# Late modulation columns and one token load moved in a fused transformer block

## The chip, the cores and the metric

The kernel runs on one core of a Trainium2 chip. The metric is the device time of one execution in microseconds; lower is better. An execution works on five engines with queues of their own: TensorE (matmul, PE), VectorE (DVE), ScalarE (ACT), GpSimd (POOL), and SyncE (SP), which here only issues DMAs. An engine starts its instructions in the order of its queue; semaphores order the engines among each other.

## The reference, cut to what matters

One transformer block over 2048 tokens of width 1024, with all its modulation computed from one condition vector `c`:

```python
mod = (silu(c) @ w_mod).reshape(1, 6, 1, -1)       # w_mod: 1024 x 6144
sa, ca, ga, sb, cb, gb = six rows of 1024
h = layernorm(x) * (1 + ca) + sa
q = (h @ wq), 32 heads of 128                       # wq: 1024 x 4096
p = softmax(q @ k.T * 128**-0.5)                    # the last 512 keys, 4 key heads
x = x + ga * ((p @ v) @ wo)                         # wo: 4096 x 1024
h = layernorm(x) * (1 + cb) + sb
x = x + gb * ((silu(h @ w_gate) * (h @ w_up)) @ w_down)   # width 3584
```

Everything is bfloat16 outside, with float32 sums.

## The kernel before, in words

The tokens are cut into four chunks of 512. Attention runs over 128 items, an item being one head of one chunk: item i belongs to chunk i // 32 and head i % 32. The loop at line 1007 writes the program out in order, and every engine gets its instructions in that order. In turn i it emits the query projection of item i + 3 (eight matmuls into one PSUM bank, then VectorE's cast to SBUF, line 675), the scores of item i - 1 (four matmuls into four banks, then the exponential on ScalarE, line 848), and the value product of item i - 2 (16 small matmuls, then a reciprocal and a multiplication on VectorE, lines 866 and 869). SP then transposes the product by DMA (line 872) into `oT_all`, from which the output projection reads it. From item 34 on, every second item takes another form: scores with queries on the partitions (line 909), normalisation on VectorE (lines 915 and 919), a transposing DMA of the probabilities (line 925), and a value product that lands transposed (line 936).

At a seam, the end of turns 33, 65 and 97, the chunk that is through gets its output projection, `oproj`: eight blocks k of 32 matmuls each, one matmul per head, into two banks in turn. Matmul h of a block reads `oT_all[:, h]`. Behind each block VectorE multiplies by the gate row and adds to the residual (lines 950 and 952). The last chunk's projection is spread over the end of the loop. The gated feed-forward of all chunks follows.

The rows `gb`, `sb` and `cb` of the modulation are wanted late. They are computed on VectorE during the first chunk's projection, 128 values at a time. A "late column" m (24 of them) is a block of `w_mod` that SP loads transposed into one of four slots (`load_mt`, line 592; slot m % 4), and that VectorE multiplies by the broadcast silu(c) and sums (`mod_col`, line 601, with the instruction at line 604). The slots lie in the buffer that held chunk 0's normalised tokens. `late_cols(k)`, line 608, is called behind block k of the first projection. It runs three columns, and behind each column m it issues the load of column m + 4 into the slot that is now free. At k = 3 the first eight columns, the gate `gb`, are turned by DMA; they go out as a row at k = 4 and come back broadcast at k = 5. At k = 7 the other sixteen are copied into the modulation table (line 629) and the gain is made (line 478).

Tables in front of the loop set which turn issues which DMA. `LOADT` issues the first four late-column loads, behind the value product of its turn. `LOADX` issues the 1 MB token loads of chunks 2 and 3 at the head of a turn; these tokens are wanted when the layer norm of their chunk starts, two turns behind a seam. `PUTT` and `GETT` store a small row to DRAM and fetch it back broadcast to all partitions; the fetch waits for the store. Query weights (1 MB, `load_wq`, line 363) are loaded every four items. All of these, like all transposes, stand in SP's one queue.

Of the kernel before, what the change touches and what calls it, by code (L numbers as in the profile page):

```python
# [130 lines left out]
def bass_adaLN_cond__sliding_block_cached__swiglu_ffn__prompt_kernel(  # L131
# [17 lines left out]
    Hq = HD // Dh  # L149
# [117 lines left out]
    with nc.Block() as block:  # L267

        @block.gpsimd
        def _(g):  # L270
# [82 lines left out]
            def wq_slot(gidx):  # L353
                return gidx if gidx <= NWQ else (gidx + 1) % NWQ
# [3 lines left out]
            def load_wq(gidx):  # L358
                if gidx >= NCH * HG:
                    return  # L360
                sl = wq_slot(gidx)
                hg = gidx % HG
                T.op(Q_wq[sl], lambda: SP.dma_start(
                    wq_s[sl], A_wq[:, hg * 512:(hg + 1) * 512].rearrange("(k p) n -> p k n", p=P)), writes=B_wq[sl])
# [219 lines left out]
            NL = NJ - NF  # L584
            NMT = 4
# [6 lines left out]
            def load_mt(m):  # L592
                sl = m % NMT
                n = L_ORDER[m]
                if mt[sl] is None:
                    mt[sl] = arena.at(OFF_HT + 2 * sl * KB, [D], BF16, [B_mt[sl]])
                T.op(Q_mt[sl], lambda: SP.dma_start_transpose(
                    mt[sl].rearrange("p (a b) -> p a b", a=1), w_mod[:, (NF + n) * P:(NF + n + 1) * P]),
                     writes=[B_mt[sl]])

            def mod_col(m):
                sl = m % NMT
                n = L_ORDER[m]
                T.op(DVE, lambda: V.scalar_tensor_tensor(mt[sl], mt[sl], 1.0, sc_row, op0=ALU.mult, op1=ALU.mult,  # L604
                                                         accum_out=mcol[:, n:n + 1]),
                     reads=[B_scr], writes=[B_mt[sl], B_mcol])

            def late_cols(k):
                for m in range(3 * k, 3 * k + 3):
                    mod_col(m)  # L610
                    if m + NMT < NL:
                        load_mt(m + NMT)
                if k == 3:
                    T.op(DVE, lambda: V.tensor_copy(mstg[:, 0:DT], mcol[:, 2 * DT:3 * DT]), reads=[B_mcol], writes=[B_mstg])
                    row_turn()
                if k == 4:
                    row_put(2, mrow[0:DT, :], B_mrow)
                if k == 5:
                    row_get(2, rowb[1][:, :], B_row[1])
                if k == 7:  # L620
                    for g0 in range(2):
                        mod_take(g0, B_late[g0 + 1])
                    mod_gain(1, B_late[2], B_g[1])
                    for b_ in B_hT[0]:
                        for m_ in B_mt:
                            b_.absorb(m_)

            def mod_take(g0, cbuf):
                T.op(DVE, lambda: V.tensor_copy(mod_bf[:, NF + g0 * DT:NF + (g0 + 1) * DT], mcol[:, g0 * DT:(g0 + 1) * DT]),
                     reads=[B_mcol], writes=[cbuf])  # L630
# [7 lines left out]
            def row_put(r, src, sbuf):  # L638
                T.op(Q_dr[r], lambda: SP.dma_start(d_rows[r:r + 1, :].rearrange("o (k p) -> (o k) p", p=P), src),
                     reads=[sbuf], writes=[B_dr[r]])  # L640

            def row_turn():
                T.op(Q_turn, lambda: SP.dma_start_transpose(mrow.rearrange("p (a b) -> p a b", a=1), mstg),
                     reads=[B_mstg], writes=[B_mrow])

            def row_get(r, dst, dbuf):
                rep_ap = bass.AP(tensor=d_rows.tensor, offset=r * D, ap=[[0, P], [1, D]])
                T.op(Q_rw[r], lambda: SP.dma_start(dst, rep_ap), reads=[B_dr[r]], writes=[dbuf])
# [344 lines left out]
                ln2[ch] = ln_task(ch, h2s[s], B_h2[s], 1, 3 * DT, B_late[1])  # L993
                bg.append(ln2[ch])

            LOADX = {19: 2, 40: 3}
            GATEP = {4: (0, 1), 5: (2,), 6: (3,), 7: (4,), 9: (5,), 10: (6,), 12: (7,), 13: (8,), 15: (9,)}
            GATER = {19 + n: NGP + n for n in range(DT - NGP)}
            GATET = {23: 0, 24: 1}
            GATES = {26: 0, 27: 1}  # L1000
            PUTT = {22: (0, c_sil, B_csil), 30: (1, mrow[0:DT, :], B_mrow)}
            GETT = {25: (0, sc_row, B_scr), 31: (1, rowb[0][:, :], B_row[0])}
            LOADT = {30: 0, 31: 1, 32: 2, 33: 3}
            LOADO = {5 + (21 * p) // 8: p for p in range(8)}
            LOADK = {1: 1, 5: 2, 6: 3}
            PTAT = {NAT0: OFF_H20, 3 * Hq: OFF_HT}
            for i in range(1, NA + 2):
                ch, h = divmod(i, Hq)
                if i in LOADK:
                    load_k(LOADK[i])  # L1010
                if i == 4:
                    load_wq((i + 4) // 4 + 1)
                if 2 <= i < NQ0:
                    q_shifted(i)
                if i in (2, 3):
                    load_wga(i - 2)
                if i in LOADX:
                    load_x(LOADX[i])
                if i in LOADO:
                    load_wo(LOADO[i])  # L1020
                if i in GATET:
                    gate_turn(GATET[i])
                if i == 28:
                    row_turn()
                if i in PUTT:
                    row_put(*PUTT[i])
                if i in GETT:
                    row_get(*GETT[i])
                if i == 7:
                    add_ln1(1)  # L1030
                if h == 2 and 1 <= ch < NCH - 1:
                    add_ln1(ch + 1)
                if h == 2 and ch == NCH - 1:
                    add_ln2(0)
                if i + LEAD < NA:
                    if (i + LEAD) % Hq == 0:
                        finish(ln1[(i + LEAD) // Hq])
                    if i == 1:
                        scores(0)
                    if i in (1, 3, 5):  # L1040
                        q_bias_mm(i + 1, i + 3, XB)
                    if i > NQ0:
                        qproj(i + LEAD)
                    elif i % 2 == 1:
                        qproj_mm(NQ0 + i // 2, QB, 0, HK)
                    else:
                        qproj(NQ0 - 1 + i // 2, QB, HK)
                if i % 4 == 0 and i > NAT0:
                    load_wq(i // 4 + 2)
                n = i - (NA - LEAD)  # L1050
                if 0 <= n <= 2:
                    oproj_mm(NCH - 1, 0, QB, 8 * n, 8 * n + 8)
                elif n >= 3:
                    oproj_mm(NCH - 1, 1, XB, 8 * (n - 3), 8 * (n - 3) + 8)
                seam = (i - 1) % Hq == 0 and i + 1 in NAT
                if i + 1 in PTAT and not seam:
                    pt_region(PTAT[i + 1])
                if i in NAT and (i - 2) % Hq:
                    nat_norm(i, 1)
                nat = i % 2 == 1 and i + 1 in NAT  # L1060
                if nat and not seam:
                    run_bg(1)
                    nat_scores(i + 1)
                if 1 <= i - 1 < NA and i - 1 not in NAT:
                    scores(i - 1)
                if 0 <= i - 2 < NA:
                    if i - 4 in pt_of:
                        nat_pv(i - 4)
                    if i in NAT and (i - 2) % Hq:
                        nat_turn(i)  # L1070
                    if i - 2 not in NAT:
                        pv(i - 2)
                    if nat and not seam:
                        nat_norm(i + 1, 0)
                    ch2, h2 = divmod(i - 2, Hq)
                    if i % 4 == 1 and 5 < i < NAT0:
                        load_wq((i + 4) // 4 + 1)
                    if i in LOADT:
                        load_mt(LOADT[i])
                    if h2 == Hq - 1 and ch2 < NCH - 1:  # L1080
                        oproj(ch2, [lambda: nat_scores(i + 1), lambda: (nat_norm(i + 1, 0), nat_norm(i + 1, 1))],
                              [n for n in sorted(pt_of) if n // Hq == ch2])
                        if seam:
                            if i + 1 in PTAT:
                                pt_region(PTAT[i + 1])
                            nat_turn(i + 1)
                if not nat or seam:
                    run_bg(1)
                for n in GATEP.get(i, ()):
                    gate_part(n)  # L1090
                if i in GATER:
                    gate_row(GATER[i])
                if i in GATES:
                    gate_sum(GATES[i])
                if i == max(GATER):
                    gate_split()
# [154 lines left out]
```

## Time and profile before

| what | value |
|---|---|
| three runs, median (lowest to highest) | 1273.71 us (1272.12 to 1275.35) |
| the profiled execution's own time | 1273.79 us |
| its span, first to last instruction | 1271.9 us |
| mean granted TensorE clock | 0.999 |
| VectorE, late columns (line 604) | 24 of 1222 ns, 29.3 us busy, first at 146.6, last at 198.4 |
| SP, transposed late-column loads (line 597) | 24, issue 1160 / 1169 / 2885 ns (least, median, most), landing 3.3 / 3.7 / 6.7 us after the start of issue |
| SP, attention transposes into `oT_all` (line 872) | part of 109 transposes from and into the arena, 3.9 us to landing |
| token loads of 1 MB (line 308) | 3, issued at 26.6, 90.7 and 222.1, landing 7.0, 7.1 and 6.0 later |
| first seam's projection | first residual addition (line 950) at 145.28, last at 194.42 |

Busy time is the time in which an engine works on an instruction. The view of waits lists who stood idle and which instruction ended the wait (total, times, longest). The chain of waits is followed back from the last instruction. In the timeline a DMA's issue stands in SP's queue with the time that the issuing took; when the data land is told apart from it. The windows view gives, for each stretch, its length, the busy time (and instructions) of PE, PEld, DVE, ACT and POOL, then the granted clock, the DMA share and GB/s.

### The profile page before, as it was taken

Reading aid. Unit: us, or ns where it says so; the run is one execution under the profiler, and the core shown is the slowest. Engines: PE = TensorE matmul, PEld = TensorE weight load, DVE = VectorE, ACT = ScalarE, POOL = GpSimd, SP = SyncE. Lnnn points to the kernel's source line nnn. Section 1 sums busy time; section 2 is a strip of 40 time slices with the busy share of each in tenths; the row PEclk is TensorE's granted clock in tenths of the full one; section 3 lists DMA queues with packets and bytes.
Section 4 is the critical chain, followed back from the end, with each engine's and each line's share of the span. In section 5 each row is a group of like instructions: output and inputs, shape, how many; then the busy total and the mean of one; then the engine's idle time right before and its main releaser. Section 6 shows DMA issues by size and latency. Waiting matters only on the chain.

```text
span 1271.9 us, 17309 instructions
## 1 busy us (share of the span) xinstructions
PE 1263.1 (99%) x7019; PEld 617.1 (49%) x7019; DVE 518.9 (41%) x1081; ACT 392.7 (31%) x718; POOL 55.9 (4%) x95
## 2 busy tenths in 40 slices
PE   9999999999999999999999999999999999999999
PEld 5655544555445554455544444444444444444444
DVE  5676577664246652376422321233212331222222
ACT  4655304775037771177710111011100111011100
POOL 1530000000000000000000000000000000000000
PEclk9999999999999999999999999999999999999999
DMA  9999666987029872099543973055411644035200
GB/s 313 266 269 222 151 132 132 216 186 151 18 41 201 168 179 41 1 191 195 99 146 100 289 223 117 25 156 151 149 58 57 191 141 132 17 118 164 67 9 26
DMA packets 312191, 175.14 MB, mean 138 GB/s; under 512 B 205488, under 2 KB 298032, under 8 KB 312112
## 3 DMA queue, kind: packets, MB, share of 16 engines
q1 hardware_dynamic: 253856, 115.31, 40.0%
q10 hardware_dynamic: 58256, 58.73, 14.6%
q8 instruction: 55, 0.90, 0.3%
q14 instruction: 24, 0.20, 0.1%
HBM read 119.93 MB, written 4.20 MB: 98 GB/s over the span
## 4 chain that ended last, share of the span: by engine, by line
PE 98%; DVE 1%; DMA 0%; issue 0%; ACT 0%; DVEq 0%; ACTq 0%
PE ps L277 98%; DVE st L430 0%; DVE arena L604 0%; DMA x_res<-in_A_x_dram 0%; DVE arena L869 0%; PE ps L281 0%; DVE arena L675 0%; ACT tmp L909 0%; DVE arena L701 0%; DVE tmp L950 0%; DVE nsc L441 0%; DVE tmp L919 0%; DVE x_res L952 0%; DVE mv L530 0%; DVE rl L866 0%
## 5 line engine op out<-in xcount | busy, mean ns | idle before, releaser
L277 PE MATMUL ps<-arena 128*128 128x512 bf16 (+1 forms) x6774 | 1257.1, 348 | 6.1 <-DVE arena L675 3.1
L277 PEld LDWEIGHTS ps<-arena 128*128 128x128 bf16 x6774 | 608.4, 98 | 648.7 <-issue 5.3
L848 ACT ACTIVATE arena<-ps 128x1024 bf16<-128x1024 f32 x160 | 163.7, 1023 | 229.9 <-PE ps L277 222.5
L1179 ACT ACTIVATE arena<-ps 128x512 bf16<-128x512 f32 x112 | 66.9, 597 | 501.0 <-PE ps L277 498.1
L1180 DVE TENSOR_TENSOR arena<-ps,arena 128x512 bf16<-128x512 f32 x112 | 77.4, 691 | 276.2 <-PE ps L277 276.2
L950 DVE TENSOR_TENSOR tmp<-ps,rowb 128x512 f32<-128x512 f32 (+1 forms) x65 | 44.4, 683 | 292.2 <-PE ps L277 292.2
L675 DVE CAST arena<-ps 128x512 bf16<-128x512 f32 x120 | 82.8, 690 | 77.9 <-PE ps L277 77.9
L909 ACT ACTIVATE arena<-ps 128x512 bf16<-128x512 f32 x96 | 56.9, 595 | 26.3 <-PE ps L277 21.9
L909 ACT ACTIVATE tmp<-ps 128x512 bf16<-128x512 f32 x92 | 54.5, 595 | 25.8 <-PE ps L277 21.6
L869 DVE TENSOR_TENSOR arena<-ps,rl 128x512 bf16<-128x512 f32 x81 | 56.0, 691 | 3.0 <-DVE rl L866 0.2
L435 POOL TENSOR_SCALAR rstd<-mv 128x1 f32<-128x1 f32 x28 | 6.1, 216 | 913.5 <-DVE mv L434 913.5
L866 DVE RECIPROCAL rl<-ps 128x4 f32<-128x4 f32 x81 | 14.7, 182 | 73.9 <-PE ps L277 73.9
L430 DVE BATCH_NORM_STATS2 st<-x_res 128x6 f32<-128x512 bf16 x62 | 42.4, 683 | 3.5 <-DMA x_res<-in_A_x_dram 3.4
L919 DVE TENSOR_SCALAR arena<-arena,pinv 128x512 bf16<-128x512 bf16 x96 | 33.9, 353 | 3.4
L936 ACT ACTIVATE arena<-ps 128x512 bf16<-128x512 f32 x47 | 27.8, 592 | 19.6 <-PE ps L277 19.6
L919 DVE TENSOR_SCALAR tmp<-tmp,pinv 128x512 bf16<-128x512 bf16 x92 | 32.5, 353 | 3.3
L604 DVE SCALAR_TENSOR_TENSOR arena<-arena 128x1024 bf16<-128x1024 bf16 x24 | 29.3, 1222 | 1.7
L952 DVE TENSOR_TENSOR arena<-tmp,x_res 128x512 bf16<-128x512 f32 (+2 forms) x33 | 22.3, 676 | 1.1
L952 DVE TENSOR_TENSOR x_res<-tmp,x_res 128x512 bf16<-128x512 f32 x32 | 22.1, 692 | 1.1
L446 DVE TENSOR_SCALAR arena<-arena,gain,mod_bf 128x512 bf16<-128x512 bf16 x56 | 21.2, 420 | 0.0
L441 DVE TENSOR_SCALAR nsc<-x_res,mv,rstd 128x1024 bf16<-128x1024 bf16 x30 | 19.2, 641 | 0.0
L909 ACT ACTIVATION_READ_ACCUMULATOR arena<-ps 128x1 f32 x96 | 18.9, 197 | 0.0
(67 smaller groups left out, 149.4 us busy)
## 6 DMA issues: line engine op xcount, KB each, us to landing
arena<-in_A_wq_dram SPq DMA_DIRECT2D x30, 1024.0 KB, 6.0
arena<-in_B_w_gate_dram ACTq DMA_DIRECT2D x28, 1024.0 KB, 5.5
arena<-in_B_w_up_dram ACTq DMA_DIRECT2D x28, 1024.0 KB, 8.2
arena<-in_A_wo_dram SPq DMA_DIRECT2D x8, 1024.0 KB, 7.6
arena<-in_B_w_down_dram SPq DMA_DIRECT2D x7, 1024.0 KB, 8.5
out_dram<-arena SPq DMA_DIRECT2D x15, 256.0 KB, 2.0
x_res<-in_A_x_dram SPq DMA_DIRECT2D x3, 1024.0 KB, 7.0
arena<-in_w_mod_dram SPq DMA_DIRECT2D x8, 256.0 KB, 5.8
```

What stands on the lines that cost most here:

```text
L277: T.op(PE, lambda: TE.matmul(out_ap, lhsT, rhs, start=start, stop=stop, skip_group_check=skip), reads=reads, writes=[bank_buf])
L430: T.op(DVE, lambda: V.bn_stats(st_[sl][:, hf * 6:hf * 6 + 6], x_res[:, t, hf * 512:hf * 512 + 512]), reads=[B_x[t]], writes=[B_st[sl]])
L604: T.op(DVE, lambda: V.scalar_tensor_tensor(mt[sl], mt[sl], 1.0, sc_row, op0=ALU.mult, op1=ALU.mult, accum_out=mcol[:, n:n + 1]), reads=[B_ ...
L675: T.op(DVE, lambda: V.tensor_copy(qT_s[qs], bank(b)), writes=[PB[b], B_qT[qs]])
L848: T.op(ACT, lambda: A.activation(ex_s[es][:, 2 * kp:2 * kp + 2, :], banks2(SCB + 2 * kp), AF.Exp, scale=att_scale), writes=[PB[SCB + 2 * k ...
L869: T.op(DVE, lambda: V.tensor_tensor(o_s[os_].rearrange("p (a b) d -> p a b d", a=2), psap(PVB * 512, [[512, 2], [130, 2], [1, P]]), rlb, A ...
L909: T.op(ACT, lambda: A.activation(pn[s][:, j * 512:(j + 1) * 512], bank(SCB + j), AF.Exp, scale=att_scale, accum_out=psum[s][:, j:j + 1]), ...
L919: T.op(DVE, lambda: V.tensor_scalar(pj, pj, pinv[s][:, j:j + 1], None, op0=ALU.mult), reads=[B_pinv[s][hf]], writes=[B_pn[s][hf]])
L950: T.op(DVE, lambda: V.tensor_tensor(tmp[s][:, 0:n], bank(b, n), rowb[ri][:, c0:c0 + n], ALU.mult), reads=[B_row[ri]], writes=[PB[b], B_tmp ...
L952: T.op(DVE, lambda: V.tensor_tensor(dst[:, c0:c0 + n], tmp[s][:, 0:n], x_res[:, t, c0:c0 + n], ALU.add), reads=[B_tmp[s], B_x[t]], writes= ...
L1179: T.op(ACT, lambda: A.activation(sg_s[ss], bank(gb), AF.Silu), writes=[PB[gb], B_sg[ss]])
L1180: T.op(DVE, lambda: V.tensor_tensor(guT[:, ft, :], bank(ub), sg_s[ss], ALU.mult), reads=[B_sg[ss]], writes=[PB[ub], B_gu[ft]])
```

## The change

- `late_cols(k)` no longer does anything behind block 7. Block 0 runs four columns (2 to 5), blocks 1 to 6 three each (6 to 8, up to 21 to 23). The copies into the modulation table and the gain move from block 7 to block 6.
- Columns 0 and 1 run in turns 32 and 33 of the item loop, behind the query projection and ahead of the scores, each followed at once by the load of column m + 4 (4 and 5).
- `LOADT` starts one turn earlier: loads 0 to 3 go out in turns 29 to 32 instead of 30 to 33.
- `LOADX` moves the token load of chunk 3 from turn 40 to turn 65, the turn of the second seam.

```diff
+            def late_col(m):
+                mod_col(m)
+                if m + NMT < NL:
+                    load_mt(m + NMT)
+
             def late_cols(k):
-                for m in range(3 * k, 3 * k + 3):
-                    mod_col(m)
-                    if m + NMT < NL:
-                        load_mt(m + NMT)
+                if k < 7:
+                    for m in range(3 * k + (3 if k else 2), 3 * k + 6):
+                        late_col(m)
...
-                if k == 7:
+                if k == 6:
                     for g0 in range(2):
                         mod_take(g0, B_late[g0 + 1])
...
-            LOADX = {19: 2, 40: 3}
+            LOADX = {19: 2, 2 * Hq + 1: 3}
...
-            LOADT = {30: 0, 31: 1, 32: 2, 33: 3}
+            LOADT = {29: 0, 30: 1, 31: 2, 32: 3}
...
                 if i % 4 == 0 and i > NAT0:
                     load_wq(i // 4 + 2)
+                if i in (Hq, Hq + 1):
+                    late_col(i - Hq)
                 n = i - (NA - LEAD)
```

## The prediction

> **What bounds the kernel now.** The page first: TensorE is busy 1263.1 of 1271.9 us, and the clock row of the slices is 9 throughout. What is left to win is TensorE's idle time, plus what a slower clock behind such a pause costs.
>
> ```profile
> PE 1263.1 (99%) x7019; PEld 617.1 (49%) x7019; DVE 518.9 (41%) x1081; ACT 392.7 (31%) x718; POOL 55.9 (4%) x95
> ```
>
> The view of waits, for TensorE alone, says where the idle time lies. Of the 8.8 us, 3.0 lie in the first 46 us and 2.4 behind the last matmul, untouched. The longest of the others is 2.9 us on line 675, VectorE's cast of a projected query from PSUM.
>
> ```profile
> PE ps L277 <- DVE arena L675: 3.1, 2, 2.9
> ...
> PE ps L277 <- ACT tmp L909: 0.2, 1, 0.2
> PE ps L277 <- DVE pinv L915: 0.2, 1, 0.2
> ```
>
> The chain of waits says why that cast was late (start, duration, what):
>
> ```profile
> 194.42 0.70 DVE tmp L950
> ...
> 195.15 0.69 DVE x_res L952
> 195.84 1.16 DVE arena L604 x2
> ...
> 199.69 0.25 DVE mod_bf L629 x2
> ...
> 200.05 0.69 DVE arena L675
> 200.74 0.05 issue
> 200.79 5.29 PE ps L277 x28
> ```
>
> Block 7 of the first output projection ends at 194.40. VectorE adds it to the residual, then runs the last three late columns (line 604) and the copies behind them, and only then casts item 37's query, from 200.05. Item 38's projection needs that PSUM bank, so TensorE stands still for 2.91 us, from 197.88 to 200.79. The windows view, cut where the granted clock changes, shows the aftermath: after a stretch with TensorE busy 0.63 of 3.42 us, the next runs at clock 0.50 and gets through eight matmuls.
>
> ```profile
> 197.25:200.67 3.42, 0.63 (x12) 0.45 (x8) 3.25 (x9) 1.38 (x2) 0.00 (x0) 1.00 0.00 0
> 200.67:204.08 3.41, 3.29 (x8) 1.19 (x9) 1.44 (x4) 0.00 (x0) 0.00 (x0) 0.50 0.20 38
> ```
>
> **Part 1, the stall removed.** The change leaves block 7 without a column. VectorE's queue after that block is then 0.69 + 0.69 (lines 950, 952) to 195.84, and the cast of item 37 follows as soon as its projection, eight matmuls after 194.4, is out: about 196.15 to 196.85, ahead of the 197.88 at which TensorE wants the bank. Gain 2.91. The eight matmuls behind it took 427 ns each in the slow window; at full clock a block of 32 takes 6.91 us (line 950 at 187.51 and 194.42), 216 ns each, so 8 x 0.211 = 1.69 more. What is late next there? The scores of item 36 need ScalarE to have emptied the four score banks (two exponentials, 196.58 to 198.72); TensorE reaches them at 197.88 + 1.73 = 199.6. That is 0.9 us of cover. The 0.16 us wait on line 915 at 208.7 is VectorE catching up after the stall; bounds 0 and 0.16, and I take it all, since VectorE will be 4 us ahead there.
>
> The Trainium skill ("TensorE: Matmul & The Clock Gate", Part 1) has the clock fall after a whole idle window of about 3.4 us. Here 2.91 us of idling, within one 3.42 us stretch that was not wholly idle, were followed by clock 0.50. By the page's rule the 1.69 would not be recovered and the sum below would be -1.7; the row decides.
>
> **Part 2, two columns before the seam.** Columns 0 and 1 move to items 32 and 33, ahead of the normalisation of items 30 and 31 in VectorE's queue. A column is 1.22 and its accumulator read, 1.25 in a row of them. In these items VectorE idles 0.82 and 1.08 us per head (line 675 and line 866 rows), so the column fits but for 0.2 us, and 0.7 if its weights land at 134.2 (below). TensorE's next value product starts near 137.4, and the line 869 that frees its banks ended at 135.72: 1.7 us of cover. Cost nothing; with the cover gone, 1.25 a column. POOL has nothing queued there: it idles for 104.2 us up to 205.96. Blocks 0 to 6 then carry 4 + six times 3 columns. Block 0 needs 1.4 + 5.0 and block 6 1.4 + 3.8 + 0.4 us of VectorE, within 6.91. Block 1 adds item 34's normalisation (1.8) to 1.4 + 3.8, about 0.1 over, covered by the alternating bank.
>
> **Part 3, SP's queue before the first seam.** This is the cost that matters. Transposed weight loads (line 597) are issued by SP in order, and the attention transposes (line 872) stand between them.
>
> ```profile
> 126.54 1.50 SPq L363 DMA_DIRECT2D arena<-in_A_wq_dram  x1
> 128.09 0.48 SPq L639 DMA_DIRECT2D mod_rows<-arena  x1
> 128.75 1.20 SPq L872 DMA_TRANSPOSE arena<-arena  x1
> 129.99 1.92 SPq L597 DMA_TRANSPOSE arena<-in_w_mod_dram  x1
> 133.73 0.36 SPq L648 DMA_DIRECT2D rowb<-mod_rows  x1
> 134.13 1.20 SPq L872 DMA_TRANSPOSE arena<-arena  x1
> 135.38 1.30 SPq L597 DMA_TRANSPOSE arena<-in_w_mod_dram  x1
> 136.72 1.26 SPq L872 DMA_TRANSPOSE arena<-arena  x1
> 138.03 1.30 SPq L597 DMA_TRANSPOSE arena<-in_w_mod_dram  x1
> 139.37 1.26 SPq L872 DMA_TRANSPOSE arena<-arena  x1
> ```
>
> The last line is item 31's transpose, out 0.1 us after its data were ready; it landed 2.5 us later, at 141.9. From the row fetch at 133.73 on, SP has no pause: it is the bound already. Block 0 needs it for its 32nd matmul, near 145.05 (line 950 starts at 145.28), so slack is 3.1 us. Now load 0 goes out right behind the query weights at 128.1, and loads 3, 4 and 5 are issued ahead of item 31's transpose too. The row fetch waits for the little row store of line 639, which landed with the query weights (issue 126.54, landing 6.8 later: 133.3) at 133.7. It now stands behind load 0 also, and the load that went out right behind query weights at 141.30 landed 0.84 after them: so 133.3 + 0.84 + 0.35 = 134.5. From there: 0.40 (fetch) + 1.25 (item 29) + 2 x 1.34 (loads 2, 4) + 1.31 (item 30) + 2 x 1.34 (loads 3, 5) = 8.32, so item 31's transpose goes out at 142.9 instead of 139.4. Its landing, 2.5 (its own row) to 3.4 us (item 30's), comes at 145.4 to 146.3. TensorE waits 0.35 to 1.25; I take 0.75. Outer bounds: 0 if the fetch is not delayed and the landing is quick; 2.0 with the slowest such landing here, 4.0 us (item 29's). In both, load 4 waits for column 0 (done by 135.5) and load 5 for column 1 (138.6); SP reaches them at 137.5 and 141.5: no wait. Load 0's buffer was last read by item 31's projection, cast from 119.48: no wait either.
>
> **Part 4, the last tokens.** The 1 MB load of chunk 3 leaves item 40 (issue 222.13, landing 6.0 later). Behind it stands the 0.2 us wait on line 909 at 235.7; bounds 0 and 0.21, I take 0.21. It arrives at item 65, ahead of item 63's transpose in SP's queue:
>
> ```profile
> 305.46 0.54 SPq L363 DMA_DIRECT2D arena<-in_A_wq_dram  x1
> 306.75 4.41 SPq L925 DMA_TRANSPOSE arena<-tmp  x1
> 311.25 1.22 SPq L872 DMA_TRANSPOSE arena<-arena  x1
> ```
>
> That last one landed 2.5 later, at 313.7; block 0 of chunk 1 needs it near 317.0 (its line 950 starts at 317.23). Now the 1 MB load goes out at 311.2 and lands at 317.2 (6.0, as at 222.13). The transpose behind cannot overtake it: chunk 2's load at 90.75 took 7.1 us, and the transpose issued 0.68 behind it landed 0.7 after it. So 317.2 + 0.6 to 0.7 = 317.8: a wait of 0.8. Bounds: 0.3 (load 5.7, as quick query weights) to 2.5 (load 7.1, transpose 1.26 behind, as at 114.91). The tokens themselves are wanted 55 us later. These two waits are far shorter than 2.91; the trace has a pause of 0.5 us (10.67 to 11.16) at full clock and nothing between. I charge no slow clock, 1.7 each at worst.
>
> **The sum.** -2.91 - 1.69 - 0.16 - 0.21 + 0.75 + 0.8 = -3.4 us. The profiled execution took 1273.79, its span 1271.9 with 1.9 around it, and the runs' median is 1273.71, so both bases agree: 1270.3. Nothing under 0.3% (3.8 us) can be told from no change here.
>
> **Rivals.**
> *No new wait (0.23).* Both transposes land in time, as their 3.1 and 3.3 us of slack might allow if the DMA queues run faster than the rows say: 1273.79 - 4.97 = 1268.8. Against it: SP's row of issues has no pause to give back.
> *SP's queue stretches (0.15), slower.* The load at 141.30 behind 1 MB of query weights took 2.88 us to issue, not 1.34. Should loads 1 to 5 all go out so, since SP now pushes six of them into the same ring, item 31's transpose is 5 x 1.54 = 7.7 later than forecast; TensorE waits 8.4 and pays a slow window: -4.97 + 8.4 + 1.7 + 0.8 = +5.9, 1279.7. It turns slower once that wait passes 2.5 us, slow window included. For it: 1.92 and 2.88 in the rows; against: three loads in a row during the projection took 1.16 to 1.17 each, with no 1 MB load among them.
> *Another wait takes the cast's place (0.10).* ScalarE's exponentials or VectorE's next casts hold TensorE as long, the clock falls as before, and only the two small waits are gained: 1273.79 - 0.37 + 1.55 = 1275.0. Against: the 0.9 us of cover, and no wait in the same rhythm at 236 to 400 us, where TensorE is busy 164.0 of 164.0.
>
> The forecast has 0.52, its own range being 1269.0 to 1272.0. Faster by over 0.3% means under 1269.9: the first rival and not quite half of the forecast, 0.46. Slower by over 0.3%: nearly all of the second, 0.14. The rest is 0.40. The range runs from 1267.8 (first rival less 1 us between runs) to 1275.0 (third rival) and leaves out the second.
>
> **What would show it.** Part 1: no line 604 between lines 952 and 675 at the end of the first seam, no clock under 1.00 after the start. Part 3: item 31's transpose near 142.9, and a TensorE wait on it at 145 us. Part 4: a 1 MB load near 307 to 311 and a wait of under 1 us before block 0 of chunk 1. Wrong would be a slow window at the first seam, or a VectorE wait for a weight load near 134.

## The result, and the profile after

Over 22 executions of each kernel on one chip the change took the median from 1273.77 to 1271.26 us: 0.9979 of the time before, 95% interval 0.9972 to 0.9985. That is 2.5 us less (1.9 to 3.6 by the interval), inside the range, on the side of the forecast, and 1.0 us above the 1270.3 forecast. As a share it is 0.21%, so of the three outcomes that were given chances it is the one under 0.3% either way (0.40), and not the likeliest, faster by more than that (0.46). The profiled execution took 1270.27, its span 1268.4: against the profiled execution before, 3.5 us less. Why these two differences are not the same is a question for the experiments.

The page's first row, after:

```profile
PE 1261.8 (99%) x7019; PEld 616.7 (49%) x7019; DVE 519.9 (41%) x1081; ACT 392.9 (31%) x718; POOL 56.3 (4%) x95
```

The view of waits, TensorE alone (total, times, longest): the cast is gone from it, and a DMA inside the arena has come in, twice.

```profile
PE ps L277 <- DMA arena<-arena: 1.2, 2, 0.7
PE ps L277 <- DVE arena L502: 0.5, 1, 0.5
```

VectorE's timeline at the end of the first seam. Line numbers behind 607 have moved by 4 to 6: 679 is the cast, 954 and 956 are the residual, 870 and 873 the normalisation, 876 and 929 the transposes of the two forms.

```profile
194.11 0.17 DVE L478 TENSOR_SCALAR gain<-mod_bf 128x8 bf16<-128x8 bf16 x1
195.47 0.69 DVE L954 TENSOR_TENSOR tmp<-ps,rowb 128x512 f32<-128x512 f32 x1 [1.19 <-PE ps L277]
196.19 0.69 DVE L956 TENSOR_TENSOR x_res<-tmp,x_res 128x512 bf16<-128x512 f32 x1
197.19 0.69 DVE L679 CAST arena<-ps 128x512 bf16<-128x512 f32 x1 [0.31 <-PE ps L277]
198.97 0.18 DVE L870 RECIPROCAL rl<-ps 128x4 f32<-128x4 f32 x1 [1.08 <-PE ps L277]
```

The cast waits for TensorE now (0.31), not TensorE for the cast. The windows view over the stretches that held the pause and the slow clock before:

```profile
197.25:200.67 3.42, 3.42 (x29) 2.04 (x28) 2.11 (x4) 2.05 (x2) 0.00 (x0) 1.00 0.00 0
200.67:204.08 3.41, 3.41 (x29) 2.08 (x28) 3.01 (x8) 2.64 (x8) 0.79 (x2) 1.00 0.20 41
```

Both are full, at clock 1.00. What came in is in SP's timeline ahead of the first seam:

```profile
126.76 0.97 SPq L363 DMA_DIRECT2D arena<-in_A_wq_dram  x1
127.77 2.27 SPq L597 DMA_TRANSPOSE arena<-in_w_mod_dram  x1
...
134.09 0.36 SPq L652 DMA_DIRECT2D rowb<-mod_rows  x1
134.50 1.20 SPq L876 DMA_TRANSPOSE arena<-arena  x1
135.74 2.65 SPq L597 DMA_TRANSPOSE arena<-in_w_mod_dram  x2
138.43 1.26 SPq L876 DMA_TRANSPOSE arena<-arena  x1
139.74 2.64 SPq L597 DMA_TRANSPOSE arena<-in_w_mod_dram  x2
142.42 2.10 SPq L876 DMA_TRANSPOSE arena<-arena  x1
```

The last line is item 31's transpose, at 142.42 instead of 139.37, landing 3.4 us after that, at 145.8. And ahead of the second seam:

```profile
306.90 0.57 SPq L308 DMA_DIRECT2D x_res<-in_A_x_dram  x1
307.56 1.19 SPq L876 DMA_TRANSPOSE arena<-arena  x1
```

The 1 MB load landed at 312.8 (5.9 later), item 63's transpose behind it at 313.3 (5.8 later). TensorE's timeline has both waits in brackets, the first at the seam of chunk 0, the second at that of chunk 1:

```profile
145.83 2.33 PE L277 MATMUL ps<-arena 128*128 128x512 bf16 x10 [0.66 <-DMA arena<-arena]
```

```profile
313.38 2.98 PE L277 MATMUL ps<-arena 128*128 128x512 bf16 x13 [0.57 <-DMA arena<-arena]
```

Where the time went between the two profiled executions is read from one operation at a time, by how much later or earlier it starts than before. These are block 0's residual at the first seam and item 63's reciprocal, before and then after (VectorE's timeline):

```profile
145.28 0.69 DVE L950 TENSOR_TENSOR tmp<-ps,rowb 128x512 f32<-128x512 f32 x1 [6.07 <-PE ps L277]
309.33 0.18 DVE L866 RECIPROCAL rl<-ps 128x4 f32<-128x4 f32 x1 [0.21 <-PE ps L277]
```

```profile
146.33 0.69 DVE L954 TENSOR_TENSOR tmp<-ps,rowb 128x512 f32<-128x512 f32 x1 [6.90 <-PE ps L277]
305.16 0.18 DVE L870 RECIPROCAL rl<-ps 128x4 f32<-128x4 f32 x1 [0.21 <-PE ps L277]
```

VectorE's cast at 126 is 0.21 late (126.05 to 126.26), a difference from the start of the execution. Block 0's residual at the first seam is 1.05 late (145.28 to 146.33): the wait for item 31 cost 0.84, its 0.66 of idling and 0.18 more behind it. Item 63's reciprocal is 4.17 early (309.33 to 305.16): the stretch from that residual to this reciprocal, the first seam with the small waits behind it, gave 5.22. Block 0's residual at the second seam is 3.42 early (317.23 to 313.81): item 63 cost 0.75. The last matmul ends 3.42 early (1269.44 to 1266.02). So 0.21 + 0.84 - 5.22 + 0.75 = -3.42.

### The profile page after: what moved, and what is told of

It is laid out like the page before. It is cut to its first block, busy times and chain, and to the rows that moved or that the text cites. A ratio compares the mean times of both kernels' runs of the same rounds, so it can differ in the third digit from the quotient of the medians.

```text
span 1268.4 us, 17308 instructions
## 1 busy us (share of the span) xinstructions
PE 1261.8 (99%) x7019; PEld 616.7 (49%) x7019; DVE 519.9 (41%) x1081; ACT 392.9 (31%) x718; POOL 56.3 (4%) x95
## 4 chain that ended last, share of the span: by engine, by line
PE 98%; DMA 1%; SPq 1%; DVE 0%; issue 0%
PE ps L277 97%; DMA arena<-arena 1%; DMA arena<-in_w_mod_dram 0%; SPq L597 0%; SPq L315 0%; DVE arena L873 0%; SPq L340 0%; PE ps L281 0%; DVE arena L604 0%; SPq L929 0%; DVE arena L679 0%; SPq L308 0%; DVE arena L502 0%; DVE rl L870 0%; DVE tmp L954 0%
```

## The experiments

All against the kernel before on the same chip; medians in us. "Clock" is the mean granted clock of an execution, and 0.999 is one step at half speed in 1272 us. The first row sets the kernel before against itself, and shows how far two medians of one kernel can differ: 0.4 us.

| kernel | median (executions) | before (executions) | ratio, 95% interval | clock 1.000 |
|---|---|---|---|---|
| before, again | 1274.18 (11) | 1274.61 (24) | 0.9994, 0.9985 to 1.0002 | 5 of 11 |
| columns only | 1270.83 (8) | 1274.61 (24) | 0.9976, 0.9966 to 0.9986 | 8 of 8 |
| tokens only | 1275.30 (11) | 1274.61 (24) | 1.0008, 0.9999 to 1.0017 | 1 of 11 |
| loads behind the transposes | 1268.99 (5) | 1274.61 (24) | 0.9958, 0.9945 to 0.9972 | 5 of 5 |
| two columns behind block 7 | 1271.29 (6) | 1275.02 (16) | 0.9971, 0.9960 to 0.9983 | 6 of 6 |
| four columns behind block 7 | 1275.94 (11) | 1275.02 (16) | 1.0010, 1.0001 to 1.0019 | 0 of 11 |
| the change, again | 1271.10 (8) | 1273.71 (12) | 0.9976, 0.9966 to 0.9986 | 8 of 8 |
| loads behind, again | 1268.41 (5) | 1273.71 (12) | 0.9956, 0.9944 to 0.9969 | 5 of 5 |
| loads behind, weights early | 1268.51 (5) | 1273.71 (12) | 0.9955, 0.9942 to 0.9969 | 5 of 5 |

### Before, again: does every execution pay the slow clock?

No edit.

> The kernel before, unchanged, run many times, with the granted clock of each execution. The two profiled executions differ by 3.5 us, the medians of 22 executions only by 2.5. Theory A (the slow clock comes by chance): TensorE's 2.91 us pause at the first seam falls differently into the fixed 3.41 us steps in which the clock is granted, so only some executions show a mean clock of 0.999 (one step at half speed, 1.7 us), the others 1.000, and those are 1.5 to 2 us shorter. Theory B (every execution pays it, and the profiled one after the change was a quick one by its start): all executions show 0.999.

Its profile has the same pause, 2.91 us from 199.04 to 201.96, and no slow step at all. The windows view, cut at the steps of the clock (they are 3.413 us long and counted from the row in which the clock rose; in the three profiles that have a slow step at this seam, before, tokens only and four columns, it begins 194.56 us behind that row, 57 such steps):

```profile
196.90:200.31 3.41, 2.15 (x22) 1.38 (x20) 3.20 (x6) 2.05 (x2) 0.00 (x0) 1.00 0.44 72
200.31:203.72 3.41, 1.76 (x9) 0.83 (x10) 2.90 (x9) 0.00 (x0) 0.00 (x0) 1.00 0.00 0
203.72:207.14 3.42, 3.37 (x28) 2.06 (x28) 2.69 (x7) 2.64 (x8) 0.79 (x2) 1.00 0.20 41
```

The pause fell across a boundary, 1.26 us into one step and 1.65 into the next, and the clock did not fall. The next step, the third line, is at 1.00 too. The clock rose 6.11 us after the first instruction in the profile before and 5.75 in this one, so the steps fall differently on the same program. Of the 63 executions of the kernel before that stand in the table, 14 have 1.000 and 49 less. On this chip the nine at 1.000 have a median of 1273.04, the 23 at 0.999 of 1274.60: 1.56 apart, where eight slow matmuls are worth 1.69. The profiles give the same size: from block 0's residual at the first seam to item 63's reciprocal it is 164.05 us before (145.28 to 309.33) and 162.49 here (146.45 to 308.94), 1.56 less. Theory A holds, theory B falls; the shares of the spans are not as clean as expected (1273.41 at 0.999 is shorter than 1274.37 at 1.000), so something else spreads the executions too.

### Two and four columns behind block 7

```diff
-                for m in range(3 * k, 3 * k + 3):
+                LC = [0, 3, 6, 9, 12, 15, 18, 22, 24]     # four: [..., 18, 20, 24]
+                for m in range(LC[k], LC[k + 1]):
```

> The kernel before with one late column moved from block 7 to block 6 (4 and 2 columns behind them). The pause at the seam shrinks by one column, 1.3 us, from 2.91 to 1.6 us. Theory A: so short a pause never fills enough of a 3.41 us step, all executions show clock 1.000, and the kernel gains 1.3 us and the share of 1.7 us that the slow step costs on average: 2 us or more. Theory B (each pause that is long costs a slow step, whatever the phase): a slow step remains in the profile and only 1.3 us are gained.

> The kernel before with one late column moved from block 6 to block 7 (2 and 4 columns behind them). The pause grows by 1.3 us to 4.2 us. Theory A: it is longer than a 3.41 us step, so nearly all executions show 0.999 and the kernel loses 1.3 us plus what part of the 1.7 us was not yet paid on average: 1.5 to 2.5 us. Theory B: 1.3 us lost.

The pauses in the profiles are 1.6 and 4.3 us, one column less and one more (view of waits, with two behind block 7 and with four):

```profile
PE ps L277 <- DVE arena L676: 1.6, 1, 1.6
```

```profile
PE ps L277 <- DVE arena L676: 4.3, 1, 4.3
```

With two behind, all six executions have clock 1.000 and the kernel gains 0.0029, 3.7 us (2.2 to 5.1): more than the 1.3 of theory B. The sum of theory A, 1.3 and some 1.3 of slow clock, lies inside the interval; the other 1 us is not accounted for. One column moved by one block thus gains no less than the whole change (0.9979 and 0.9976), as far as these runs can tell, and adds nothing to SP's queue ahead of item 31's transpose. With four, none of the 11 reaches 1.000; four of them have 0.996 or 0.997, two steps or more. It loses 1.3 us (0.1 to 2.4), under the 1.5 to 2.5 expected, and its time alone does not tell A from B; the clocks do. The windows view of the kernel with four:

```profile
198.46:201.87 3.41, 0.00 (x0) 0.00 (x0) 3.24 (x8) 0.22 (x1) 0.00 (x0) 1.00 0.00 0
201.87:205.29 3.42, 3.20 (x8) 1.16 (x9) 1.54 (x4) 0.00 (x0) 0.00 (x0) 0.50 0.20 38
```

A step without a single matmul, and the next one at half speed with eight.

### Columns only, tokens only

Columns only is the change with the tokens' table as it was; tokens only is the kernel before with

```diff
-            LOADX = {19: 2, 40: 3}
+            LOADX = {19: 2, 2 * Hq + 1: 3}
```

> The spread of the late columns with its earlier loads, but the last tokens loaded in turn 40 as before. If the parts add up as in the two traces (seam 5.2 gained, 0.84 lost on item 31's transpose, 0.75 lost on item 63's), this one has the first two: its profile shows no wait at the second seam, a wait of 0.6 to 0.7 us near 145, and it is 0.75 us shorter than the change as a whole, less up to 0.2 us at 235: 0.9974 of the kernel before. Rival: the columns' seam gains nothing without the move of the tokens, then 1.000.

> The kernel before with the last tokens' load moved to turn 65, nothing else. By the theory that item 63's transpose waits behind 1 MB: a TensorE wait of 0.5 to 0.8 us before the end of block 0 of chunk 1's projection, the stall of 2.9 us at the first seam unchanged, at most 0.2 us gained near 235: 1.0004 of the kernel before (0.5 us longer). Rival: the move is what the change gains by, with the DMA queue relieved behind the first seam; then 0.999 or less.

The columns bring all of the gain that can be seen: 0.9976, and no wait at the second seam. That it is 0.75 us shorter than the whole change was expected too; the change did not run on this chip, and the ratios (0.9976, and 0.9976 and 0.9979 for the change) do not show it. The expectation for 145 us missed in size. This program is the same as the change's up to there, yet its profile has (TensorE's timeline)

```profile
146.45 3.84 PE L277 MATMUL ps<-arena 128*128 128x512 bf16 x17 [1.68 <-DMA arena<-arena]
```

with item 31's transpose out at 143.68 instead of 142.42, mostly because load 5 ahead of it took 2.04 us to issue and not 1.30. The size of this wait is a matter of the execution.

The tokens alone bring nothing. The first seam's pause is there (2.9), and the new wait comes where it was expected. SP's timeline and the view of waits:

```profile
307.14 4.33 SPq L925 DMA_TRANSPOSE arena<-tmp  x1
311.53 0.57 SPq L308 DMA_DIRECT2D x_res<-in_A_x_dram  x1
312.19 1.19 SPq L872 DMA_TRANSPOSE arena<-arena  x1
```

```profile
PE ps L277 <- DVE arena L675: 2.9, 1, 2.9
...
PE ps L277 <- DMA arena<-arena: 0.6, 1, 0.6
```

The load lands at 317.4, the transpose at 317.9. The ratio, 1.0008 with 1.0 inside its interval, is on the side of a loss without settling it; the wait itself is shown.

### Loads 4 and 5 and the tokens behind the transposes

```diff
             def late_col(m):
                 mod_col(m)
-                if m + NMT < NL:
+                if 2 <= m and m + NMT < NL:
                     load_mt(m + NMT)
...
-            LOADX = {19: 2, 2 * Hq + 1: 3}
+            LOADX = {19: 2}
...
                     if i in LOADT:
                         load_mt(LOADT[i])
+                    if i == Hq + 1:
+                        load_mt(4)
+                        load_mt(5)
+                    if i == 2 * Hq + 1:
+                        load_x(3)
```

> The change, with loads 4 and 5 issued behind item 31's transpose (and behind the query weights that follow it) instead of ahead of it, and the last tokens' load behind item 63's transpose. If the queue order is what costs the two waits, item 31's transpose goes out near 139.7 and lands near 142.5, no TensorE wait is left at 145 and at the second seam, and the kernel gains 0.84 + 0.75 = 1.6 us on the change: span 1266.8, 0.9966 of the kernel before. Rival: the waits are the DMA engines' own, full with other transfers; then item 31's transpose still lands after 145 and at most half of it is gained.

> Loads 4 and 5 and the last tokens behind the transposes, once more, beside the change on one chip. By the queue theory no wait at 145 us and none at the second seam in this profile either, and a median 1.4 to 2.2 us under the change's. Rival (the order at the seams is worth nothing, the first run was a quick chip): within 0.6 us of it.

Both seams are free of TensorE waits for a transpose in both profiles. The view of waits of the second run, whole but for its heading:

```profile
PE ps L277 <- POOL arena L304: 2.0, 1, 2.0
PE ps L277 <- DVE arena L502: 0.6, 1, 0.6
PE ps L277 <- DMA arena<-in_w_mod_dram: 0.2, 1, 0.2
PE ps L277 <- issue: 0.2, 1, 0.2
```

Its SP timeline, first seam and second:

```profile
139.13 1.30 SPq L597 DMA_TRANSPOSE arena<-in_w_mod_dram  x1
140.47 1.26 SPq L876 DMA_TRANSPOSE arena<-arena  x1
141.83 1.81 SPq L363 DMA_DIRECT2D arena<-in_A_wq_dram  x1
143.69 7.59 SPq L597 DMA_TRANSPOSE arena<-in_w_mod_dram  x4
```

```profile
305.96 1.22 SPq L876 DMA_TRANSPOSE arena<-arena  x1
307.23 0.57 SPq L308 DMA_DIRECT2D x_res<-in_A_x_dram  x1
```

Item 31's transpose goes out at 140.47, 0.8 later than expected, and lands at 144.7, 2.2 later than expected and 0.3 before it is needed. In the first run, where block 0's residual comes 1.9 us later than in the kernel before (147.14), it went out at 141.59 and landed at 146.1, 0.8 before it was needed. The second run's issue comes 2.0 and 2.3 us earlier than those in the two profiles of the change (142.42 and 142.80), but the landing takes 4.2 us (4.5 in the first run) instead of 3.4: the order in the queue removes the wait, and why the landing takes longer was not shown. On one chip the median is 2.7 us under the change's (1268.41 to 1271.10), more than the 1.4 to 2.2 expected, the span 1266.6. The first run's profile has a 1.6 us wait of another kind, for query weights at 121 us, ahead of everything that was edited:

```profile
PE ps L277 <- DMA arena<-in_A_wq_dram: 1.6, 1, 1.6
```

### The change, again

> The changed kernel, unchanged, on the same chip as the next two. Its profile shows how far its own waits vary from execution to execution: 0.66 us on item 31's transpose in its first profile, 1.7 in that of the columns alone, which issues the same up to there. If that is chance, this one lies between 0.5 and 1.8 us there, and 0.5 to 0.7 us at the second seam. All its executions have clock 1.000.

```profile
PE ps L277 <- DMA arena<-arena: 2.3, 2, 1.2
```

1.21 us on item 31's transpose (at 145.06) and 1.05 on item 63's (at 313.25; expected was 0.7 at most). With 0.18 more behind each (block 0's residual comes 1.39 and 1.23 later than without a wait) these are 2.6 us; the loads behind the transposes are 2.7 faster on the same chip.

### Query weights early

```diff
+                if i % 4 == 1 and 5 < i < Hq:        # at the head of the turn
+                    load_wq((i + 4) // 4 + 1)
...
-                    if i % 4 == 1 and 5 < i < NAT0:
+                    if i == Hq + 1:
                         load_wq((i + 4) // 4 + 1)
```

> As the one before, with the query weights of turns 9 to 29 issued at the head of their turn instead of behind the value product's transpose. Four of the profiles so far show TensorE waiting 0.2 to 1.6 us for query weights at 107, 121 or 135 us, which land within 1 us of their need. Theory: this is what spreads the executions of one kernel over 2 to 3 us; the weights then land 2 to 3 us earlier, no such wait is left, the spread falls under 1.2 us, and the median is 0.3 to 0.8 us lower than without. Rival: the load ahead of the transposes delays them and what waits for them, then it is no faster.

The weights of turn 25 went out at 111.2 and landed at 116.9 instead of 120.5, item 31's transpose landed at 142.1, and no wait for query weights is in the profile. The median is the same as without (1268.51 and 1268.41): the rival's time, though not its mechanism, since the transposes were not delayed. The spread is 0.7 us over five executions, against 1.4 over five; too few to call it narrower, and the profile without the edit had no such wait either. What it buys is room at the first seam, some 3 us in place of 0.3 (item 31's transpose is needed 0.2 us before block 0's residual, which starts at 145.75 here and at 145.25 without).

## Why the prediction was right

*The bound and the stall.* The cast behind block 7 was the bound there, and it is gone; nothing took its place. Forecast 4.97 us for the first seam and the two small waits behind it (2.91, 1.69, 0.16, 0.21), read off the traces 5.22. The run of the kernel before without a slow step splits this: from block 0's residual to item 63's reciprocal it takes 162.49, the change 158.83 in both of its profiles. These 3.66 stand against 3.22 of idling in that run (2.91, 0.16, 0.15), so the waits cost 0.44 more than their idling. The other 1.56 are the slow step, but for 0.06 by which the wait at 235 us was longer before. The third rival, another wait in the cast's place, is out: TensorE is busy 3.42 of 3.42 us there.

*The clock.* The slow step is real, at some 1.5 us for 1.69 forecast, but not in every execution: 49 of 63 have one or more. The prediction charged it as if every execution paid. The same 2.91 us pause costs a step or none by how it falls on the steps: one with 2.56 us of idling was enough, one with 1.65 was not. The first of these, from tokens only, and the step that followed:

```profile
197.91:201.32 3.41, 0.85 (x16) 0.68 (x12) 3.17 (x8) 1.60 (x2) 0.00 (x0) 1.00 0.00 0
201.32:204.73 3.41, 3.06 (x8) 1.14 (x9) 1.68 (x4) 0.00 (x0) 0.00 (x0) 0.50 0.20 38
```

The Trainium skill ("TensorE: Matmul & The Clock Gate", Part 1) describes a window of about 3.4 us that runs freely and does not start anew with the kernel; the steps of 3.413 us here agree. Its rule that the clock falls after an idle window, taken as a wholly idle one, differs from the step with 2.56 us of idling, and the step decides.

*Two columns before the seam.* Without cost, as reckoned. VectorE's rows in the changed kernel run without a gap from column 0 (133.86, 1.22) to item 30's reciprocal at 135.03, which is where it stood before (134.81) once the 0.21 from the start are taken off: the column fills the gap exactly. TensorE has no wait between 126 and 145. A column in a row takes 1.33 us from start to start in the rows before (188.85, 190.18, 191.51), not the 1.25 of the prediction; the blocks had room for that, and TensorE has no wait from 145.83 to 198.0.

*SP's queue before the first seam.* Item 31's transpose was forecast at 142.9, landing at 145.4 to 146.3; measured 142.42 and 145.8, then 142.80 and 146.2, and 143.68 and 146.4 (the last in columns only). The 8.32 summed from the row fetch on held in the two profiles of the change, 8.33 and 8.31, and was 9.33 where load 5 was slow. That the loads ahead of it in the queue make the wait was shown by taking two of them out; what sets the time to landing (2.4 to 4.5 us for this transpose over the profiles) was not. The slack of 3.1 us was that of one execution: in tokens only, which issues like the kernel before up to here, the transpose went out at 141.49 and landed at 145.6, some 0.3 before it was needed. The outer bound of 2.0 follows neither from its own figures (142.9 + 4.0 - 145.05 is 1.85) nor was 4.0 the slowest landing in the rows (item 28's took 5.2); the longest wait measured is 1.68.

*The last tokens.* Forecast: out at 311.2 and landing at 317.2 by the clock of the trace before, a wait of 0.8. In tokens only, where nothing earlier has moved, 311.5 and 317.4, and 0.57. The lower bound of 0.3 is 0.5 by its own figures (311.2 + 5.7 + 0.6 - 317.0). In all three profiles the small transpose landed 0.5 to 0.6 behind the 1 MB load ahead of it. The Trainium skill ("DMA: Bandwidth & Descriptors", Queues, rings and completion order) has each DMA engine take descriptors in ring order, but does not promise that transfers complete in the order of issue; in these three they did. The 0.21 us at 235 us, taken as a gain, is one: four of the five profiles with the load in turn 40 have a wait of 0.2 to 0.5 us there (0.32 in columns only), and none of the six with the load moved.

*The size.* The sum of -3.4 meets the two profiled executions (-3.42), partly by luck. The one before lies at its kernel's median (1273.79 against 1273.77), but the one after is 1.0 us under its own (1270.27 against 1271.26), with shorter waits than the others. Two terms of the sum were mis-sized. The two waits were taken at 0.75 and 0.8; measured over the profiles they are 0.66, 1.68 and 1.21 at the first seam (mean 1.18) and 0.57, 0.57 and 1.05 at the second (mean 0.73), each with 0.18 behind it: 2.3 together, not 1.55. In the second profile of the change they cost 2.6, 1.0 more than in the first, and its execution took 1271.17, 0.9 more, on another chip. The slow clock costs 49/63 of 1.69 on average, 1.3 us, not 1.7; a median moves by less (1274.37 over the 35 executions of the first experiment's chip, 1274.60 over those with one slow step). So -4.97 + 0.4 + 2.3 = -2.3, against -2.5 measured; with three profiles for each wait this is an estimate, and it leaves out the 0.25 that the first stretch gave beyond its forecast. The first rival, no new wait, did not come; moving the loads behind the transposes makes it true, and where it was put at 4.97 under the kernel before, that kernel is 5.3 and 5.6 under it. The second rival, a stretched queue with a slow clock, did not come; no execution of the change is under clock 1.000.

## What to carry to other kernels

Moving work earlier also moves what feeds it: count the DMA issues that now stand ahead of an urgent transfer in the same queue, and put loads that are not urgent behind it, which here was worth as much as the change itself (2.7 and 2.6 us on one chip). Look first for the smallest move: one column taken out from behind the last block gained 3.7 us (2.2 to 5.1). A pause of TensorE cost its own length and a little more here, and a slow clock step only when it filled enough of one fixed step; so one profiled execution can over- or understate a stall, and the mean clock of many executions tells which share pays.

## What was not expected of the hardware

A pause of 1.6 us never slowed the clock (6 executions of 6 with two columns behind), one of 2.9 us did in 49 of 63 (and in 10 of 11 of tokens only, which has the same pause), one of 4.3 us always (11 of 11). If the pause falls evenly over the 3.41 us steps, a share of 49/63 means that a step must be idle for about 1.8 us; this is an estimate from that share alone, between the 1.65 that did not and the 2.56 that did, and it holds only if every one of the 49 owes its slow step to this pause.

The issue of a transposing load took 1.16 to 3.3 us, and the longest ones stood behind 1 MB of query weights (2.88 to 2.93 right behind them in three profiles, 3.31 two small issues further on in tokens only); one load that took 2.0 instead of 1.3 made the wait at the first seam 1.68 us. TensorE waited 0.2 to 1.6 us for query weights in four of the first eight profiles, and the other four show no such wait.
